# List scheduling of every engine's order in a gated attention and MLP kernel, with attention started beside the projections and phi(k) transposed by DMA

## The chip, the cores and the metric

The kernel runs on one core of a Trainium2 chip. The time is device microseconds (us) of one execution, given as the median of several runs. The program gives the core five instruction streams and fixes the order of each when it is built: PE (matrix multiply; its weight loads are listed as PEld), DVE (vector), ACT (activation functions), POOL (general purpose), SP (here it only issues DMAs). They wait for each other through semaphores. "Span" is the time from the first to the last instruction of the profiled run. It is about 2 us shorter than the reported time (256.4 against 258.4 us for the kernel before).

## The reference

The output is a gated sum of an attention branch and a token-mixing MLP. Here S = 2048 tokens, D = 448, H = 16 heads of Dh = 28, N = 4 segments of L = 512 tokens, F = 1792.

```python
def _A_ref(x, wq, wk, wv, wo, beta):          # q, k, v: x @ w, split in heads and segments
    phi = lambda t: jnp.where(t > 0, t + 1.0, jnp.exp(t))
    for s in range(N):
        p = softmax(q_s @ k_s.T * scale + causal_mask)
        a_dot = p @ v_s
        a_mem = (phi(q_s) @ M) / (phi(q_s) @ z + 1e-6)
        o = g * a_mem + (1.0 - g) * a_dot      # g = sigmoid(beta), one per head
        M = M + phi(k_s).T @ v_s
        z = z + phi(k_s).sum(0)
    return o @ wo

def _B_ref(x, w1, b1, w2, b2):                 # mixes tokens: w1 is S x F, w2 is F x S
    h = layernorm(x)
    u = gelu(einsum('bsd,sf->bdf', h, w1) + b1)
    return (einsum('bdf,fs->bds', u, w2) + b2).transpose(0, 2, 1)

g = sigmoid((x * gate_w).sum(-1))
return g * a + (1 - g) * b
```

## The kernel before

The program is first recorded as a list of operations with the buffers they read and write. Semaphore waits are derived from that list. Each engine gets its operations in the order of the text, so the hand order is the schedule:

```python
    def op(self, eng, fn, reads=(), writes=(), name=None, dma=False, group=None, out=False):
        ...                                    # dependencies from reads and writes
        self.ops.append(o)
        self.per_eng[eng].append(o)            # program order is engine order
```

First come the projections, token block by token block. phi(q) takes four instructions on three engines. phi(k) is needed with tokens on partitions, and a second projection of x by wk supplies it in that layout:

```python
    def do_q(tc, hg):
        proj_d(wq_pad, R_wqp, hg, tc, b)                                        # PE, 4 matmuls
        op("DVE", lambda e: e.tensor_copy(qs, bank(b)[:, 0:512]), ...)
        op("ACT", lambda e: e.activation(eqt[:, p, :], bank(b)[:, 0:512], ACT.Exp), ...)
        op("POOL", lambda e: e.tensor_scalar(eqt[:, p, :], eqt[:, p, :], 1.0, 0.0, op0=ALU.min, op1=ALU.max), ...)
        op("DVE", lambda e: e.scalar_tensor_tensor(phq..., qs, 0.0, eqt[:, p, :], op0=ALU.max, op1=ALU.add), ...)

    def do_kt(t):
        proj_t(wk_nat, [R_wkn], D, t, b)                                        # PE, 4 matmuls: the second K projection
        op("ACT", ... ACT.Exp from PSUM); op("POOL", ... min)
        op("DVE", lambda e: e.scalar_tensor_tensor(phk..., bank(b)..., 0.0, ekt..., op0=ALU.max, op1=ALU.add), ...)

    for tc in range(4):
        ...                                    # K, memory state, Q, V, second K, layernorm statistics
        if tc == 3:
            ln_coef()
            for t in range(NT):
                ln_apply(t)                    # 16 POOL operations, in one block
```

Then come 16 attention units (segment, head group) with three score slots each. The MLP's 448 matmuls are spread evenly among the slots. Each output tile is closed by the output projection, so attention is added last:

```python
    for n in range(NSLOT + 2):
        if n < NSLOT:
            scores(n)                          # PE scores, ACT exp of up to 128 x 2048, POOL causal mask
        if n % 3 == 1 and n >= 4:
            pv_unit(n // 3 - 1)                # PE p @ v and memory term, DVE scaling and transposes
        target = total * (n + 1) // (NSLOT + 2)
        mlp(target - pos[0])                   # the next matmuls of the MLP stream
        if y_done: ...
            wo_tile(T, MISC, range(NHG))
            final(T, MISC)                     # DVE: gate * attention + (gated MLP result)
```

The softmax here doesn't subtract the row's maximum and nothing guards it: scores larger than these inputs give would overflow.

## Time and profile before

The median is 258.97 us (258.11 to 259.32, 3 runs).

| stretch of the span, us | what runs | PE busy | clock granted to PE |
|---|---|---|---|
| 11.07 to 92 | projections, phi | 62.3 of 80.9 | 0.88 |
| 92 to 106 | layernorm applied on POOL | 9.7 of 14.0 | 0.50 |
| 106 to 244 | attention and MLP | 119.6 of 138.0 | 0.97 |

From the page of the kernel before: busy time and share of the span by engine, then three rows of the 40 equal slices (each digit is tenths of a slice; PEclk is the clock that the profile shows as granted to PE, in tenths of full speed), then the engines of the chain that ended last (followed back from the last instruction, at each step to what released it).

```profile
PE 201.7 (79%) x1377; PEld 90.4 (35%) x1389; DVE 147.3 (57%) x265; ACT 140.5 (55%) x180; POOL 83.3 (32%) x122
...
PE   0499994996795028998989984995889898899893
...
POOL 8001112301402099714443542340443223233000
PEclk9999998699799555589999998899999999999999
...
PE 39%; DVE 25%; ACT 18%; POOL 9%; issue 4%; DMA 3%; DVEq 0%; ACTq 0%
```

No engine is busy all the time, and the chain changes engine often. In slices 14 to 17 the clock row stands at 5: PE does almost nothing in the first two of them (0 and 2 in its row) and works at that clock in the other two (8 and 9). Next, the busy time of each engine in chosen stretches of the same run; the columns are stretch, length, busy time and instruction count per engine, granted clock, share of the DMA engines, GB/s:

```profile
core 0: us, PE busy (x) PEld busy (x) DVE busy (x) ACT busy (x) POOL busy (x), PEclk, DMA share, GB/s
0.00:11.07 11.07, 1.95 (x16) 1.75 (x16) 2.88 (x4) 1.28 (x1) 5.98 (x14) 1.00 0.87 251
11.07:92.00 80.93, 62.32 (x341) 30.04 (x341) 47.01 (x105) 33.31 (x74) 16.90 (x26) 0.88 0.31 74
92.00:106.00 14.00, 9.65 (x29) 2.05 (x30) 0.00 (x0) 2.34 (x2) 13.72 (x21) 0.50 0.00 1
106.00:244.00 138.00, 119.56 (x950) 52.46 (x961) 94.93 (x152) 101.40 (x101) 46.68 (x63) 0.97 0.28 79
244.00:256.40 12.40, 8.28 (x44) 4.09 (x42) 2.46 (x4) 2.17 (x3) 0.00 (x0) 1.00 0.11 37
```

And pieces of the chain of waits in order of time (start, duration, what). L410 is the max-add that ends phi(q). It comes back every 2.78 us, the latency of one pass through DVE, ACT, POOL and DVE again. L498 and L506 are layernorm on POOL; PE sits idle for 8.59 us before the first MLP matmul, waiting for L506.

```profile
...
41.45 0.69 DVE t L410
44.23 0.69 DVE t L410
...
90.05 2.95 POOL t L498
93.70 11.20 POOL t L506 x16
...
```

### The profile page before, as it was taken

To read this page: it belongs to the slowest core of one execution; us is meant where nothing else is said; L and a number is where in the kernel's file an instruction comes from. 1 tells how busy PE (TensorE), PEld (TensorE's weight loads), DVE (VectorE), ACT (ScalarE), POOL (GpSimd) and SP (SyncE) were. 2 spreads that over 40 slices of the span, in tenths; PEclk is the share of its full clock that TensorE was granted. 3 is DMA by queue.
4 is the path that set the end of the run, shared out by engine and by line. 5 is a ranking of instruction groups with operands and counts; after the bars stand their busy time and mean duration, and the time that the engine had idled before them with its cause. 6 is when DMAs were issued, how large, how long until landed. Compare 5 with 4: busy or idle time off the path is not lost.

```text
span 256.4 us, 3519 instructions
## 1 busy us (share of the span) xinstructions
PE 201.7 (79%) x1377; PEld 90.4 (35%) x1389; DVE 147.3 (57%) x265; ACT 140.5 (55%) x180; POOL 83.3 (32%) x122
## 2 busy tenths in 40 slices
PE   0499994996795028998989984995889898899893
PEld 0245551362352001233334431432343343334451
DVE  0426855944854700235567785974986677568703
ACT  0234614532641602389999986776766757756121
POOL 8001112301402099714443542340443223233000
PEclk9999998699799555589999998899999999999999
DMA  6999900000000000032632523145061460100102
GB/s 202 311 257 291 289 10 0 5 0 0 0 3 0 0 1 0 0 102 64 164 94 51 143 62 85 36 111 143 0 182 38 141 179 21 36 20 0 36 3 72
DMA packets 35908, 20.19 MB, mean 79 GB/s; under 512 B 1332, under 2 KB 35892, under 8 KB 35892
## 3 DMA queue, kind: packets, MB, share of 16 engines
q1 hardware_dynamic: 33328, 18.35, 26.5%
q10 hardware_dynamic: 2564, 1.62, 2.6%
q8 instruction: 11, 0.18, 0.3%
q14 instruction: 5, 0.04, 0.1%
HBM read 18.13 MB, written 1.84 MB: 78 GB/s over the span
## 4 chain that ended last, share of the span: by engine, by line
PE 39%; DVE 25%; ACT 18%; POOL 9%; issue 4%; DMA 3%; DVEq 0%; ACTq 0%
PE t L689 13%; ACT t L577 9%; PE t L374 6%; PE t L385 5%; PE t L656 5%; POOL t L506 4%; PE t L720 4%; DVE t L410 3%; DMA t<-in_A_wq_dram 3%; POOL t L408 3%; DVE t L402 3%; ACT t L406 3%; PE t L608 3%; PE t L568 2%; DVE t L728 2%
## 5 line engine op out<-in xcount | busy, mean ns | idle before, releaser
L577 ACT ACTIVATE t<-t 128x2048 bf16<-128x2048 f32 (+1 forms) x48 | 76.5, 1594 | 30.9 <-PE t L568 30.8
L656 PE MATMUL t<-t 128*128 128x448 bf16 x224 | 55.0, 382 | 10.4 <-POOL t L506 8.6
L689 PE MATMUL t<-t 128*128 128x448 bf16 x224 | 46.4, 353 | 0.0
L587 POOL TENSOR_SCALAR_AFFINE_SELECT t<-t 128x512 bf16<-128x512 bf16 x32 | 23.9, 748 | 50.4 <-ACT t L577 50.4
L582 POOL TENSOR_SCALAR_AFFINE_SELECT t<-t 128x512 bf16<-128x512 bf16 x32 | 24.2, 756 | 33.0 <-ACT t L577 31.9
L656 PEld LDWEIGHTS t<-t 128*128 128x128 bf16 x224 | 20.5, 101 | 38.0 <-issue 15.4
L374 PE MATMUL t<-t 112*128 112x512 bf16 x128 | 31.3, 401 | 3.3 <-DVE t L365 3.3
L385 PE MATMUL t<-t 112*128 112x449 bf16 (+1 forms) x112 | 26.7, 393 | 7.9 <-ACT t L406 6.5
L568 PE MATMUL t<-t 28*128 28x512 bf16 (+3 forms) x256 | 18.2, 319 | 16.1 <-ACT t L577 11.2
L689 PEld LDWEIGHTS t<-t 128*128 128x128 bf16 x224 | 20.2, 98 | 20.1 <-issue 2.6
L670 DVE SCALAR_TENSOR_TENSOR t<-t 128x448 f32<-128x448 f32 x14 | 9.2, 661 | 31.2 <-ACT t L667 31.1
L406 ACT ACTIVATE t<-t 128x512 bf16<-128x512 f32 x12 | 7.2, 597 | 27.6 <-DVE t L402 27.6
L728 DVE SCALAR_TENSOR_TENSOR t<-t 128x448 bf16<-128x448 f32 x16 | 10.5, 671 | 17.0 <-PE t L720 14.8
L408 POOL TENSOR_SCALAR t<-t 128x512 bf16<-128x512 bf16 x12 | 7.4, 613 | 38.6 <-ACT t L406 38.6
L374 PEld LDWEIGHTS t<-t 112*128 112x128 bf16 x128 | 12.9, 103 | 19.6 <-issue 3.6
L696 ACT ACTIVATE t<-t 128x448 bf16<-128x448 f32 x16 | 11.6, 722 | 14.7 <-PE t L689 14.7
L385 PEld LDWEIGHTS t<-t 112*128 112x128 bf16 x112 | 11.2, 105 | 21.4 <-DVE t L402 8.1
L410 DVE SCALAR_TENSOR_TENSOR t<-t 128x512 bf16<-128x512 bf16 x12 | 8.3, 692 | 17.9 <-POOL t L408 17.9
L568 PEld LDWEIGHTS t<-t 28*128 28x128 bf16 x256 | 5.2, 92 | 35.4 <-ACT t L577 21.8
L608 PE MATMUL t<-t 128*32 128x512 bf16 (+3 forms) x256 | 12.2, 312 | 6.8 <-DVE t L728 4.8
L429 POOL TENSOR_SCALAR t<-t 128x448 bf16<-128x448 bf16 x12 | 7.4, 616 | 25.9 <-ACT t L427 25.8
L402 DVE CAST t<-t 128x512 bf16<-128x512 f32 x16 | 11.0, 685 | 7.1 <-PE t L374 7.1
(70 smaller groups left out, 236.9 us busy)
## 6 DMA issues: line engine op xcount, KB each, us to landing
t<-in_B_w_dram SPq DMA_DIRECT2D x7, 1024.0 KB, 12.5
t<-in_B_w_dram SPq DMA_DIRECT2D x8, 896.0 KB, 5.1
t<-in_A_x_dram SPq DMA_DIRECT2D x4, 448.0 KB, 8.1
out_dram<-t SPq DMA_DIRECT2D x16, 112.0 KB, 1.7
t<-in_A_wk_dram ACTq DMA_DIRECT2D x1, 392.0 KB, 5.3
t<-in_A_wq_dram ACTq DMA_DIRECT2D x1, 392.0 KB, 7.9
t<-in_A_wv_dram ACTq DMA_DIRECT2D x1, 392.0 KB, 9.7
t<-in_A_wo_dram ACTq DMA_DIRECT2D x4, 98.0 KB
```

Source lines behind the costliest of these rows:

```text
L374: last = e.matmul(bank(b)[:, 0:512], w_pad[0:CK, c, hg * 128 : hg * 128 + 128], xT[0:CK, c, tc * 512 : tc * 512 + 512], start=(c == 0), st ...
L385: last = e.matmul(bank(b)[:, 0:ncol], xT[0:CK, c, t * 128 : t * 128 + 128], w[0:CK, c, 0:ncol], start=(c == 0), stop=(c == NCT - 1), skip_ ...
L402: op("DVE", lambda e: e.tensor_copy(qs, bank(b)[:, 0:512]), reads=[R_bank[b]], writes=[R_qT[hg][tc]], name=f"cpq{tc}_{hg}")
L410: op("DVE", lambda e: e.scalar_tensor_tensor(phq[:, hg, (tc - 1) * 512 : tc * 512], qs, 0.0, eqt[:, p, :], op0=ALU.max, op1=ALU.add), read ...
L568: last = e.matmul(bank(hl)[:, c0 : c0 + w_], kT[r, hg, s * 512 + j * 128 : s * 512 + j * 128 + 128], qT[r, hg, s * 512 + 128 * j : s * 512 ...
L577: op("ACT", lambda e: e.activation(pv, ps[:, 0:4, 0:w], ACT.Exp, scale=SCALE), reads=R_bank[0:4], writes=[R_P[u % 2][f]] + alias, name=f"e ...
L582: op("POOL", lambda e, d=d: e.affine_select(d, d, pattern=[[0, 4], [1, 128]], compare_op=ALU.is_ge, fill=0.0, base=0, channel_multiplier=- ...
L587: op("POOL", lambda e: e.affine_select(d, d, pattern=[[0, 4], [1, 128]], compare_op=ALU.is_ge, fill=0.0, base=0, channel_multiplier=-1), r ...
L608: last = e.matmul(bank(CTX)[32 * hl : 32 * hl + 32, 128 * j : 512], vaug[:, 4 * s + j, 32 * h : 32 * h + 32], pv[:, hl, c0 : c0 + w_], sta ...
L656: op("PE", lambda e: e.matmul(bank(b)[:, 0:D], w1c[:, st, f2 * 128 : f2 * 128 + 128], xh[:, st, :], start=(st == 0), stop=(st == NT - 1), ...
L689: op("PE", lambda e: e.matmul(bank(b)[:, 0:D], w2c[:, ft, t2_ * 128 : t2_ * 128 + 128], uT[:, ft, :], start=(ft == 0), stop=(ft == NFT - 1 ...
L728: op("DVE", lambda e: e.scalar_tensor_tensor(outst[:, p, :], bank(b)[:, 0:D], gcol[:, T : T + 1], ybw[:, T % 4, :], op0=ALU.mult, op1=ALU. ...
```

## The change

The intent is to let the program find its own overlap. Every operation gets an estimated cost and a priority class, and a list scheduler orders each engine for the whole kernel. On each engine it repeatedly takes the ready operation of the best class. The classes let attention go ahead of the projections, so its exps can start after the first quarter of them. The rest of the change gives the scheduler room and removes work:

- Buffers are laid out anew. The exps no longer lie over the transposed x and phi(k), nor the MLP's middle result over the projection weights. There are seven weight slots in place of five, and four of them reuse buffers of the projections and of phi(k).
- phi(k) comes from the K copy already in SBUF and is transposed by 12 DMAs, so the second K projection goes.
- The epsilon of the denominator is folded into a mask, and the sum of the two attention terms moves from DVE to POOL.
- The MLP's second half goes to the end, and its result y is added last.
- Nine warm-up matmuls run before the data arrives.

```diff
@@ the scheduler (cut)
+    def plan(self):
+        ...                                   # ready times from dependencies, one queue per engine
+            _, o = heapq.heappop(avail[e])    # lowest prio among the ready ones
+            ...
+            self.per_eng[e].append(o)         # this is the engine's order
@@ classes
+    P_BASE, P_ATT, P_PROJ, P_WO, P_M1, P_M2 = 0.0, 100.0, 200.0, 300.0, 400.0, 500.0
@@ phi(k) (cut)
-    def do_kt(t):
-        proj_t(wk_nat, [R_wkn], D, t, b)
-        ...
+    def do_kphi(tc, hg):
+        op("ACT", lambda e: e.activation(kphi[:, p, :], ks, ACT.Exp), ..., prio=P_PROJ + tc)
+        op("POOL", lambda e: e.tensor_scalar(kphi[:, p, :], kphi[:, p, :], 1.0, 0.0, op0=ALU.min, op1=ALU.max), ...)
+        op("DVE", lambda e: e.scalar_tensor_tensor(kphi[:, p, :], ks, 0.0, kphi[:, p, :], op0=ALU.max, op1=ALU.add), ...)
+        op("SP", lambda e: e.dma_start_transpose(phk[:, 4 * tc : 4 * tc + 4, hg * 128 : hg * 128 + 128],
+                                                 kphi[:, p, :]), ...)
@@ layernorm ranks ahead of the projections
+           reads=[R_x[t], R_rstd, R_nmr], writes=[R_x[t]], name=f"ln{t}", cost=580, prio=P_PROJ - 10)
@@ the sum of the attention terms
-            op("DVE", lambda e: e.tensor_tensor(o, oA[:, :], t2[:, 1, :], op=ALU.add), ...)
+            op("POOL", lambda e: e.tensor_tensor(o, t2[:, 0, :], t2[:, 1, :], op=ALU.add), ..., cost=1350, prio=pr)
@@ the end: attention is scaled early by ACT, the MLP result is added last
+        op("ACT", lambda e: e.activation(ag(T), bank(b)[:, 0:D], ACT.Identity, bias=b2g[:, T : T + 1],
+                                         scale=gcol[:, T : T + 1]), ...)
-        op("DVE", lambda e: e.scalar_tensor_tensor(outst[:, p, :], bank(b)[:, 0:D], gcol[:, T : T + 1],
-                                                   ybw[:, T % 4, :], op0=ALU.mult, op1=ALU.add), ...)
+        op("DVE", lambda e: e.scalar_tensor_tensor(outst[:, p, :], bank(b)[:, 0:D], omg[:, T : T + 1], ag(T),
+                                                   op0=ALU.mult, op1=ALU.add), ...)
@@ (buffers, loads, the remaining costs cut)
```

## The prediction

> **What bounds it now.** No single engine. The page gives a span of 256.4 us, PE busy 79%, DVE 57%, ACT 55%, POOL 32%. The chain of waits mixes PE 39%, DVE 25%, ACT 18%, POOL 9%: the order of work bounds. The busy times by stretch show three stages:
> - 0–92 us, projections. Each phi(q) is DVE copy, ACT exp, POOL min, DVE max-add, 2.78 us per tile on the chain, twelve times; PE stalls, its granted clock falls to 0.88.
> - 92–106 us, layernorm applied on POOL (11.2 us on the chain), PE nearly idle, clock 0.5: eight 448-column matmuls take 2.8–5.4 us, later 1.6. The Trainium skill, "TensorE: Matmul & The Clock Gate", section "What's actually happening", says that an idle window of about 3.4 us halves the clock; this trace agrees (0.50 here, 1.00 when busy).
> - 106–244 us, attention beside the MLP: 8.6 us per unit, 16 units; PE busy 119.6 of 138 us, ACT 101. Then 12 us of MLP and output.
>
> **What changes.** Removed: the second K projection, 48 matmuls (9 us of PE), and 12 eps adds (2.7 us of DVE). Added: 12 SBUF-to-SBUF transposing DMAs, 9 warm-up matmuls before data, 12 POOL adds of 512 f32 (the DVE sums, 9.5 us, go there). Moved: attention of segment 0 starts after a quarter of the projections; phi and layernorm fill gaps; all mm2 (224 matmuls) goes to the end, with a DVE add and a DMA behind each tile. Weight slots: five to seven.
>
> **Cost, by start-to-start times in the timeline** (0.19 us per 448-column matmul; ACT instructions overlap by 0.1 us, so exps take 1.77 and 0.93):
> - PE: MLP 448 x 0.19 = 85; projections 128 x 0.216 + 64 x 0.19 = 40; attention with memory term 30; output projection 12; transposes, state, mode changes 12. Sum 179 us.
> - ACT: exps 71.5, copies 17, phi exps 12.5, gelu 22, output scaling 10, rest 3: 136 us, about 131 before the last attention unit.
> - DVE about 115, POOL about 95 us in that stretch.
>
> **Sum.** First projection at about 9.5 us (11.1 before): x and wk arrive in smaller pieces, but a tanh of beta, whose small DMA took 9.9 us to land before, is ordered ahead of ACT's first copy. Everything up to the last attention unit is bounded by ACT (131) and PE (125) together; with 10% of stalls in fixed orders it ends near 152 us. Behind it only PE: 44 mm1 matmuls 8.4, output projection 3, mm2 42.5 us; then 3.5 us for add and DMA. Span 207–209, plus 2.5 us outside it as before.
>
> Predicted: **209 us**, range 198 to 224. Faster by over 2%: 0.96; within 2%: 0.025; slower: 0.015.
>
> **What would show it.** PE clock near 1.0 after 10 us; no PE gap over 3 us; first exp before 20 us; last exp at 145–160 us with ACT 85–90% busy until then; the last 45–55 us PE over 95% busy while ACT and POOL idle; PE busy 185–195 us; chain of waits mostly PE and ACT.
>
> **What would make it wrong.** The transposing DMAs: the skill, "VectorE: DVE Perf Modes", section "The three transpose paths", gives 1309 ns for one 128x128; no transfer in this trace shows it. They queue on SP behind 3 MB of weights; phi(k) is double-buffered, so late ones stall ACT, DVE, then PE, in order. If each takes over 5 us: 220 or more. DVE slowed by more POOL traffic (690 ns adds take up to 1.1 us now) would also lengthen the first stretch. If the fixed orders fit the chip better than I assume: 200.

## The result, and the profile after

The median is 223.85 us (222.83 to 224.56, 4 runs), against 258.54 us for the kernel before in the same rounds. The ratio is 0.8657, with a 95% interval of 0.861 to 0.8705. Ratios in this document divide the mean time of one kernel by that of the kernel before in the same rounds, so they are not quite the ratio of the quoted medians.

Some lines that follow are named by their line in the new kernel:

| line | operation |
|---|---|
| L491 | K and Q projections |
| L675, L684, L688 | scores, exp, causal mask |
| L711 | p @ v |
| L511 and L513 | POOL min and DVE max-add of phi(k) |
| L632 to L639 | layernorm (L633 is its power, L639 its application) |
| L774, L799 | first and second half of the MLP |

From the page of the new kernel, the rows that answer to those of before:

```profile
PE 194.6 (87%) x1343; PEld 86.7 (39%) x1350; DVE 145.3 (65%) x261; ACT 138.1 (62%) x181; POOL 105.8 (47%) x133
...
PE   7599696968866988958879898999999999999994
...
POOL 8120419999999567966484445455452000000000
PEclk9999999679996799985999999999999999999999
...
PE 52%; DVE 17%; POOL 16%; ACT 12%; issue 2%
```

The POOL row now holds 9s in slices 7 to 13, where it was busy for at most 4 tenths before, and is empty at the end, while the PE row ends in 9s. The stretches of the new kernel:

```profile
10.00:33.00 23.00, 20.85 (x134) 9.02 (x133) 18.56 (x57) 15.93 (x23) 4.61 (x7) 1.00 0.82 204
33.00:69.00 36.00, 26.34 (x221) 11.36 (x222) 26.45 (x42) 28.47 (x41) 34.61 (x43) 0.89 0.10 20
69.00:100.00 31.00, 26.11 (x209) 10.25 (x204) 25.03 (x37) 23.89 (x33) 23.47 (x28) 0.89 0.14 29
100.00:165.70 65.70, 61.26 (x478) 25.47 (x482) 51.39 (x80) 59.06 (x69) 36.10 (x42) 0.96 0.50 135
165.70:222.80 57.10, 53.95 (x284) 27.48 (x282) 19.54 (x29) 8.23 (x14) 1.26 (x1) 1.00 0.27 81
```

From 33 to 69 us POOL is busy for 34.61 of 36 us (fifth busy figure), while PE works only 26.34 of them at a mean clock of 0.89. After 165.7 us PE is busy for 53.95 of 57.10 us, while ACT (8.23) and POOL (1.26) are nearly idle. The last p @ v of attention ends at 165.65 us.

The timeline on POOL shows what fills it (start, duration, engine, line, operation, tile shapes, count):

```profile
34.69 2.92 POOL L633 TENSOR_TENSOR t<-t 128x16 f32<-128x16 f32 x1
...
39.38 3.24 POOL L639 TENSOR_SCALAR t<-t 128x448 bf16<-128x448 bf16 x4
42.58 0.63 POOL L688 TENSOR_SCALAR_AFFINE_SELECT t<-t 128x512 bf16<-128x512 bf16 x1
43.20 2.80 POOL L639 TENSOR_SCALAR t<-t 128x448 bf16<-128x448 bf16 x4
...
```

The power of layernorm (2.92 us) and its sixteen applications stand between the masks of attention. The p @ v of the second and of the fifth attention unit, on PE, wait for those masks (the bracket is the idle time before it and what ended it):

```profile
39.44 0.73 PE L711 MATMUL t<-t 128*32 128x512 bf16 x16 [2.36 <-POOL t L688]
...
68.84 1.25 PE L711 MATMUL t<-t 128*32 128x512 bf16 x16 [1.96 <-POOL t L688]
```

Another change shows in the groups of instructions (line, engine, operation, shapes, count, then busy us and mean ns). The max-add of phi(q), in the kernel before, and then the max-add of phi(k), in the new one:

```profile
L410 DVE SCALAR_TENSOR_TENSOR t<-t 128x512 bf16<-128x512 bf16 x12 | 8.3, 692 | 17.9 <-POOL t L408 17.9
```

```profile
L513 DVE SCALAR_TENSOR_TENSOR t<-t 128x512 bf16<-128x512 bf16 x12 | 11.4, 960 | 0.0
```

It is the same operation on the same shapes, and its mean duration went from 692 to 960 ns. The Trainium skill, "SBUF — State Buffer", section "SBUF: two separate sides", says that a DVE operation with two SBUF inputs and a GpSimd operation that reads SBUF exclude each other through a shared port for the whole instruction. This trace agrees in direction: with POOL busy beside it the operation is slower on average. One by one, the twelve took between 675 and 1750 ns, so some were not slowed although POOL was busy. The final add (L804), which has one PSUM input, takes 684 ns with POOL idle, against 671 before (L728), where POOL was partly at work.

### The profile page after: what moved, and what is told of

Same layout as the page of the kernel before. It is cut to its first block, busy times and chain, and to the rows that moved or that the text cites. A ratio compares the mean times of both kernels' runs of the same rounds, so it can differ in the third digit from the quotient of the medians. Undisturbed runs are those within 1.5% of the kernel's fastest.

```text
span 222.8 us, 3401 instructions
## 1 busy us (share of the span) xinstructions
PE 194.6 (87%) x1343; PEld 86.7 (39%) x1350; DVE 145.3 (65%) x261; ACT 138.1 (62%) x181; POOL 105.8 (47%) x133
## 4 chain that ended last, share of the span: by engine, by line
PE 52%; DVE 17%; POOL 16%; ACT 12%; issue 2%
PE t L799 19%; PE t L774 11%; PE t L491 7%; ACT t L684 6%; POOL t L639 6%; POOL t L688 5%; PE t L757 4%; PE t L545 3%; PE t L711 2%; DVE t L734 2%; DVE t L736 2%; DVE t L784 2%; PE t L675 2%; PE t L447 2%; DVE t L744 2%
## 5 line engine op out<-in xcount | busy, mean ns | idle before, releaser
L684 ACT ACTIVATE t<-t 128x2048 bf16<-128x2048 f32 (+1 forms) x48 | 77.2, 1608 | 5.4 <-PE t L675 5.3
L688 POOL TENSOR_SCALAR_AFFINE_SELECT t<-t 128x512 bf16<-128x512 bf16 x64 | 47.5, 747 | 39.2 <-ACT t L684 38.1
L774 PE MATMUL t<-t 128*128 128x448 bf16 x224 | 50.6, 359 | 2.4 <-ACT t L781 1.3
L799 PE MATMUL t<-t 128*128 128x448 bf16 x224 | 42.5, 352 | 0.0
L491 PE MATMUL t<-t 112*128 112x512 bf16 x128 | 35.8, 425 | 4.2 <-DVE t L484 2.1
L774 PEld LDWEIGHTS t<-t 128*128 128x128 bf16 x224 | 20.7, 99 | 24.2 <-issue 7.2
L804 DVE SCALAR_TENSOR_TENSOR t<-t 128x448 bf16<-128x448 f32 x16 | 10.9, 684 | 29.0 <-PE t L799 29.0
L799 PEld LDWEIGHTS t<-t 128*128 128x128 bf16 x224 | 21.9, 98 | 20.5 <-DVE t L789 0.2
L738 POOL TENSOR_TENSOR t<-t 128x512 bf16<-128x512 f32 x12 | 16.8, 1401 | 13.3 <-DVE t L736 13.3
L675 PE MATMUL t<-t 28*128 28x512 bf16 (+3 forms) x256 | 17.8, 312 | 5.8 <-ACT t L684 5.7
L491 PEld LDWEIGHTS t<-t 112*128 112x128 bf16 x128 | 12.2, 106 | 21.8 <-issue 6.8
L725 DVE STREAM_TRANSPOSE t<-t 128x512 f32<-128x512 f32 x16 | 11.3, 709 | 11.4 <-PE t L711 11.2
L711 PE MATMUL t<-t 128*32 128x512 bf16 (+3 forms) x256 | 12.7, 322 | 6.9 <-POOL t L688 6.8
L545 PE MATMUL t<-t 112*128 112x449 bf16 x64 | 15.9, 385 | 1.5 <-DVE t L524 1.3
L757 PE MATMUL t<-t 128*128 128x448 bf16 x64 | 15.1, 368 | 1.5 <-DVE t L744 1.3
L503 ACT ACTIVATE t<-t 128x512 bf16<-128x512 f32 x16 | 9.6, 605 | 8.9 <-PE t L491 8.9
L639 POOL TENSOR_SCALAR t<-t 128x448 bf16<-128x448 bf16 x16 | 14.7, 927 | 0.5 <-PE t L471 0.5
L744 DVE STREAM_TRANSPOSE t<-t 128x512 bf16<-128x512 bf16 x16 | 11.2, 703 | 4.7 <-POOL t L738 4.6
L675 PEld LDWEIGHTS t<-t 28*128 28x128 bf16 x256 | 5.2, 92 | 22.9 <-ACT t L684 16.3
L511 POOL TENSOR_SCALAR t<-t 128x512 bf16<-128x512 bf16 x12 | 9.2, 768 | 8.1 <-ACT t L509 8.1
```

Of the source, the lines that this page charges most:

```text
L491: last = e.matmul(bank(b)[:, 0:512], w_pad[0:CK, c, hg * 128 : hg * 128 + 128], xT[0:CK, c, tc * 512 : tc * 512 + 512], start=(c == 0), st ...
L545: last = e.matmul(bank(b)[:, 0 : D + 1], xT[0:CK, c, t * 128 : t * 128 + 128], wvx[0:CK, c, :], start=(c == 0), stop=(c == NCT - 1), skip_ ...
L639: op("POOL", lambda e: e.tensor_scalar(xh[:, t, :], xh[:, t, :], rstd[:, t : t + 1], nmr[:, t : t + 1], op0=ALU.mult, op1=ALU.add), reads= ...
L675: last = e.matmul(bank(hl)[:, c0 : c0 + w_], kT[r, hg, s * 512 + j * 128 : s * 512 + j * 128 + 128], qT[r, hg, s * 512 + 128 * j : s * 512 ...
L684: op("ACT", lambda e: e.activation(pv, ps[:, 0:4, 0:w], ACT.Exp, scale=SCALE), reads=R_bank[0:4], writes=[R_P[u % 2][f]], name=f"exp{n}", ...
L688: op("POOL", lambda e, d=d: e.affine_select(d, d, pattern=[[0, 4], [1, 128]], compare_op=ALU.is_ge, fill=0.0, base=0, channel_multiplier=- ...
```

## The experiments

All twelve runs gave correct results. Unless said otherwise, a run is the new kernel with the edit shown. The runs name four explanations for the time that was missed:

- **A:** POOL's backlog from 33 to 69 us holds attention up.
- **B:** DVE sets the pace after 69 us, and DVE and POOL slow each other.
- **C:** the orders are fixed from wrong durations.
- **D:** the half clock of PE costs the time.

### e1_ln_dve and e2_ln_late: layernorm off POOL, or later on POOL

```diff
 e1:
-        op("POOL", lambda e: e.tensor_scalar(xh[:, t, :], xh[:, t, :], rstd...   cost=580, prio=P_PROJ - 10)
+        op("DVE", lambda e: e.tensor_scalar(xh[:, t, :], xh[:, t, :], rstd...    cost=250, prio=P_PROJ - 10)
 e2:
-  coefficients prio=P_BASE, application prio=P_PROJ - 10
+  coefficients prio=P_PROJ + 8, application prio=P_PROJ + 9
```

> Layernorm apply (16 ops, 14.7 us on POOL) goes to DVE[...]. Theory A (POOL's backlog from 33 to 69 us, 34.6 of 36 us busy, holds up the masks and with them the attention): the last attention unit ends 5 to 9 us sooner, time 215 to 219 us. Rival B (DVE is the limit before 120 us; POOL's backlog only shifts waiting): under 2 us gained, or slower, since DVE gets more work.

> The same layernorm work stays on POOL but ranks behind phi(q) and phi(k). Theory A in the form 'it is the order on POOL': masks and phi come earlier, 2 to 6 us gained, the first MLP matmul later than 85.7 us. If it is the amount of POOL work and not its order: within 1.5 us of 223.9 or slower, because the MLP starts later and the attention stage has less to fill PE with.

e1 measured 220.78 us (ratio 0.8538, 0.8508 to 0.8568) and e2 220.75 us (0.8523, 0.8497 to 0.8548). Against the new kernel's 0.8657 that is a gain of 3.1 us for e1 (0.0119 of 258.6) and of 3.5 us for e2; from here on gains are worked out in this way, and the 95% intervals make them uncertain by about 1.5 us. Since e2 leaves all the work on POOL (34.54 of 36 us busy from 33 to 69 us), the order is enough for its gain. But the path that theory A named does not show: the last p @ v ends at 164.38 us in e1 and 165.04 us in e2, after 165.65 us, and not 5 to 9 us sooner. What ends sooner is the first half of the MLP (169.21 and 170.44 us, after 177.56 us).

### e3_o_dve and e4_min_dve: moving work between POOL and DVE

```diff
 e3:
-            op("POOL", lambda e: e.tensor_tensor(o, t2[:, 0, :], t2[:, 1, :], op=ALU.add), ...  cost=1350
+            dv(lambda e: e.tensor_tensor(o, t2[:, 0, :], t2[:, 1, :], op=ALU.add), ...           650
 e4:
-        op("POOL", lambda e: e.tensor_scalar(... 1.0, 0.0, op0=ALU.min, op1=ALU.max)  # phi(q), phi(k)
+        op("DVE", lambda e: e.tensor_scalar(... 1.0, 0.0, op0=ALU.min, op1=ALU.max)
```

> Undoes one part: the 12 sums of the two attention terms go back from POOL (16.8 us) to DVE (about 0.65 us each, 8 us in all). There is none of them before segment 1, so the stretch 33 to 69 us stays. Rival B (DVE limits 69 to 120 us, 43 of 51 us busy): 3 to 6 us slower. If POOL-DVE interference or POOL latency is what costs there, it is equal or up to 3 us faster.

> The 24 min operations of phi (18.7 us on POOL) go to DVE. Theory A: POOL's backlog shrinks by half, 3 to 7 us gained. Rival B: DVE gets 24 more instructions[...], time equal or up to 4 us slower.

e3 measured 226.03 us (0.8734, 0.871 to 0.8757): 2.0 us slower, so moving the sums to POOL was a small gain. e4 measured 221.97 us (0.8585, 0.8545 to 0.8625): 1.9 us faster. Both effects are barely clear of the noise and lie between what the two theories said. On DVE a sum took 0.85 us and a min 0.38 us. Relieving one of the two engines loads the other. POOL's busy time from 33 to 69 us fell to 24.34 us in e4 and 23.81 us in e1, from 34.61 us, without the gain that theory A expected, so POOL alone does not set the pace of that stretch.

### e5_fill: keep PE's clock up

After the plan is made, short matmuls of the identity with itself are put in front of six PE operations that wait. They write to a PSUM bank that the next operation overwrites.

```diff
     sch.plan()
+    FILL = {"pv1": (CTX, 24), "prd2_": (CTX, 14), "prd3_": (CTX, 12), "pv4": (CTX, 20), "pv7": (CTX, 16), "prt15": (None, 16)}
+    ...  last = e.matmul(bank(b)[:, 0:128], ident[:, :], ident[:, :], start=True, stop=True, ...)
```

> 102 short matmuls of the identity with itself are put into the six longest PE gaps of the new kernel between 36 and 100 us (1.0 to 1.5 us each, less than the gap), so that the activity does not fall; results unchanged. Theory D (the four stretches at half clock, 20.5 us of the trace, cost about 10 us of PE time and that is part of the missing 15 us): the half clock mostly disappears and 4 to 9 us are gained. Rival A+B (POOL until 69 us and DVE until 112 us set the pace, PE would only wait longer): the clock rises, the gaps grow, under 2 us gained.

It measured 223.81 us (0.8666, 0.863 to 0.8701), the same time, while the mean clock rose from 0.954 to 0.977. The stretches of this run, to be compared with those of the new kernel above:

```profile
10.00:33.00 23.00, 20.85 (x130) 8.73 (x129) 17.32 (x51) 15.46 (x23) 4.40 (x7) 0.88 0.81 203
33.00:69.00 36.00, 28.70 (x278) 14.86 (x276) 27.53 (x44) 29.11 (x41) 33.83 (x42) 0.95 0.10 20
69.00:100.00 31.00, 26.46 (x257) 12.41 (x258) 25.39 (x37) 24.39 (x34) 23.55 (x29) 1.00 0.15 31
```

In the last two the clock is at 0.95 and 1.00 (it was 0.89 in both), and POOL is as full as before (33.83 of 36 us). Before 33 us it fell from 1.00 to 0.88, ahead of the first added matmul (37.60 us). Counted as time at half clock, the trace has about 10 us where the new kernel had about 20. Theory D finds no support: the time did not move, give or take 1.5 us, so the low clock from 33 to 100 us cost little of its own. It is not excluded altogether, since half of that time remains, and two of the four executions had a mean clock of 0.962, which the new kernel reached too.

### e6_kt: the second K projection back

```diff
-        op("SP", lambda e: e.dma_start_transpose(phk..., kphi[:, p, :]), ...)
+        last = e.matmul(bank(b)[:, 0:512], xT[0:CK, c, t * 128 : t * 128 + 128], wk_pad[0:CK, c, :], ...)  # 4 per token tile
+        ...   # exp from PSUM, min on POOL, max-add from PSUM into phk
```

> Undoes one part: phi(k) comes from a second K projection with tokens on partitions (48 matmuls of 512 columns, 10.4 us of PE at 0.216 us) as before, in place of the 12 transposing DMAs; all else and the scheduler stay. If the removed PE work is gain on the critical path: 8 to 13 us slower. If POOL and DVE set the pace in that stretch and PE has slack: under 4 us slower.

It measured 235.71 us (0.9108, 0.9082 to 0.9133): 11.7 us slower by the ratios (0.0451 of 258.6). That fits the 10.4 us of PE work, but the run does not isolate it: the second K projection also takes PSUM banks that the scores need, and the first scores, which wait for a max-add of phi(k), come at 40.83 us where they came at 21.04 us. How the 11.7 us divide between the two is not shown.

### e7_no_overlap: projections ahead of attention

```diff
-    P_BASE, P_ATT, P_PROJ, ... = 0.0, 100.0, 200.0, ...
+    P_BASE, P_ATT, P_PROJ, ... = 0.0, 250.0, 200.0, ...
```

> Undoes one part: projections rank ahead of attention, so the exps start later; list scheduling, transposing DMAs and the order of the end stay. If the overlap of attention with the projections is the main gain: 12 us slower or more, as ACT (131 us of work before the last attention unit) starts its exps later. If list scheduling and the removed work are the main gain: within 5 us of 223.9, since the MLP can fill PE beside attention as before.

It measured 217.21 us (0.8402, 0.8376 to 0.8429): 6.6 us faster than the new kernel, which lies outside both expectations. The part of the change that should have been its main gain costs time when the rest is in place. Starting attention early adds its masks and its DVE work to the stretch in which POOL and DVE already carry phi and layernorm (from 33 to 69 us POOL is busy 34.61 us in the new kernel and 29.38 us here). That this is the reason is argued, not tested. The first MLP matmul, which could keep PE busy, comes at 85.66 us in the new kernel and at 75.65 us here.

This run has a fault of its own. In its timeline POOL runs twelve layernorm applications in a row (8.75 us), the max-add of phi(k) on DVE has waited 8.86 us for POOL when it starts, and PE has waited 7.61 us for DVE:

```profile
...
37.47 8.75 POOL L639 TENSOR_SCALAR t<-t 128x448 bf16<-128x448 bf16 x12
...
46.84 2.86 DVE L513 SCALAR_TENSOR_TENSOR t<-t 128x512 bf16<-128x512 bf16 x1 [8.86 <-POOL t L511]
...
50.35 1.89 PE L491 MATMUL t<-t 112*128 112x512 bf16 x4 [7.61 <-DVE t L524]
...
```

### e8_recost: plan with the measured durations

```diff
-  ln 580, phi min 627, phi max-add 683, power 250, oa 650, om 650, garg 630
+  ln 900, phi min 760, phi max-add 930 and 880, power 2920, oa 790, om 750, garg 720
```

> The scheduler plans with the durations that the profile of the new kernel shows in place of its own guesses: layernorm apply 0.90 us for 0.58, phi min 0.76 for 0.63, phi max-add 0.93 and 0.88 for 0.68, the power 2.92 for 0.25, the two scalings of attention 0.79 and 0.75 for 0.65, gelu argument 0.72 for 0.63. Theory C (orders fixed from too short durations cause the stalls): 3 to 8 us gained. Rival: the amount of work per engine and its rank set the pace, not the guesses: within 2 us.

It measured 226.36 us (0.8759, 0.874 to 0.8778), 2.6 us slower. Theory C falls in this form. The stretch from 33 to 69 us did improve:

```profile
33.00:69.00 36.00, 31.52 (x265) 13.37 (x263) 25.56 (x44) 34.88 (x52) 32.31 (x43) 0.98 0.08 16
```

PE is busy for 31.52 us (26.34 in the new kernel), and the first MLP matmul comes at 67.63 us. But the projections now last until 110.29 us (101.35 before), and between 100 and 140 us PE is busy for 32.00 us after 35.92. Better durations alone did not give a better order under these classes. With the classes of e7 or e9 they were not run, so that rival stays open.

### e9_noov_lnlate and e10_noov_lndve: e7 with layernorm moved

```diff
 e9 = e7 + e2,   e10 = e7 + e1
```

> e7 and e2 together: projections rank before attention, and layernorm apply ranks behind phi(q) and phi(k) on POOL. Theory E (in the run without overlap, POOL's pow and 12 layernorm ops from 33.5 to 46.2 us hold phi(k), DVE for 8.9 us and PE for 7.6 us): that gap goes, 209 to 213 us. Rival (the MLP needs all of layernorm, so later layernorm means a later first MLP matmul than 75.7 us, and that sets the time): 215.5 to 220 us.

> e7 and e1 together: projections first, layernorm apply on DVE (it took 0.56 us each there, 8.1 us in all, for 12 to 15 us on POOL). Theory E: the gap of 7.6 us goes and layernorm is over earlier, 208 to 213 us. Rival (DVE is then the pace, it has 27.6 of 31 us already from 69 to 100 us): 215 us or more.

e9 measured 215.8 us (0.8342, 0.832 to 0.8363), a further 1.5 us, and is the best of the variants that keep the new operations. e10 measured 219.05 us (0.8472, 0.8451 to 0.8493), 1.8 us slower than e7. The rival's number was closer both times. Its mechanism for e9 was not: the first MLP matmul came at 72.57 us, sooner than in e7 (75.65 us). The wait of 7.6 us shrank to 5.3 us in e9, so theory E was only half put to the test there. In e10 it is gone (no wait of PE for another engine exceeds 2.9 us), and the time rose all the same.

### e11_sched_only: the scheduler alone, on the old operations

Everything of the kernel before stays: its operations, shared buffers, second K projection and evenly spread MLP. The order of every engine changes, DMA issues included. The new `finalize` comes along and drops waits that others already cover, so that the trace has 63 semaphore instructions where it had 125; what that alone is worth was not run. The new `plan` is put in, the priority of an operation is its place in the hand order, and the costs are taken from the durations in the profile of before or from the new kernel's cost helpers.

```diff
-        self.per_eng[eng].append(o)                 # hand order
+        prio = len(self.ops)                        # hand order is only the priority
+        cost, mode, nbytes = guess(eng, name, dma)
...
+    sch.plan()
     totals = sch.finalize()
```

> The kernel before with one part of the change alone: its own operations, buffers and second K projection, but the order of each engine from the new list scheduler, with the hand order as priority. If list scheduling by itself brings most of the gain: 235 us or less. If the gain comes from freeing the operations from one another (own buffers and banks, less PE work, phi from SBUF copies, layernorm not in one block): above 248 us.

It measured 207.3 us (207.17 to 207.75; ratio 0.8022, 0.8004 to 0.8041). That is 51 us less than the kernel before and 16.4 us less than the whole change (0.0635 of 258.5). It still has the PE work of the second K projection. From its page, with the stretches below:

```profile
PE 190.5 (93%) x1389; PEld 88.0 (43%) x1389; DVE 149.6 (73%) x265; ACT 139.3 (68%) x180; POOL 84.0 (41%) x122
...
PE   0699999999988999999999989899999999999992
...
POOL 8300304589996244334534442542342341432000
PEclk9999999999999999999999999999999999999999
...
```

```profile
8.60:66.70 58.10, 56.49 (x337) 29.19 (x337) 46.63 (x100) 30.62 (x71) 30.87 (x43) 1.00 0.47 114
66.70:190.00 123.30, 120.69 (x977) 51.36 (x978) 94.43 (x151) 104.63 (x107) 46.69 (x65) 1.00 0.31 89
190.00:205.40 15.40, 11.35 (x61) 5.68 (x58) 5.85 (x11) 2.89 (x4) 0.00 (x0) 1.00 0.10 31
```

PE is busy 56.49 of 58.10 us during the projections (62.3 of 80.9 before), because other work now fills the passes through DVE, ACT and POOL. All of it belongs to the projections and the memory state: the first score matmul starts at 66.74 us and the first MLP matmul at 67.40 us. The applications of layernorm run from 45.56 to 63.43 us, beside the projections, and no longer in a block behind them. Of the 51 us, about 37 are gained here (94.93 us from 11.07 to 106 us before, 58.10 now). PE is busy 120.69 of 123.30 us during attention and MLP, with the clock at 1.00 throughout; that stretch took 138 us before. POOL is busy 30.87 of those 58.10 us; in the same stretch of the new kernel it is busy 36.93 us and PE 47.37. Then PE-heavy MLP and ACT-heavy attention run side by side to the end, and ACT is busy 104.63 of 123.30 us.

The groups of this run also show the two forms of phi's max-add side by side. L552 has two SBUF inputs, L573 takes one of its inputs from PSUM:

```profile
L552 DVE SCALAR_TENSOR_TENSOR t<-t 128x512 bf16<-128x512 bf16 x12 | 10.1, 866 | 2.5 <-POOL t L550 2.5
L573 DVE SCALAR_TENSOR_TENSOR t<-t 128x448 bf16<-128x448 f32 x12 | 7.3, 613 | 2.5 <-POOL t L571 2.5
```

In the kernel before, the PSUM form took 622 ns, so it is undisturbed here (613), while the SBUF form is again slowed (866, from 692).

### e12_mix: the old mix of MLP and attention, with the new operations

This is e9, with the MLP ranked evenly among the attention units rather than behind them.

```diff
-               prio=P_M1 + ft)                      -  prio=P_M2 + T)                 -  pr = P_WO + T
+               prio=P_ATT + 16.5 * i / 408.0)       # i: place in the stream of 448   +  pr = P_ATT + T + 4.6
```

> The run with projections first and layernorm late (215.8 us), with one thing changed: the MLP matmuls no longer rank behind all attention but are spread evenly among the 16 attention units, as the hand order had them, and each output projection ranks behind its own unit. Operations, buffers and transposing DMAs are those of the new kernel. Theory F (what the new kernel loses against list scheduling of the old operations, 207.3 us, is the ranking: attention in front starves PE, then PE runs alone for 57 us): 203 to 209 us, PE clock 1.0 after 75 us, no PE-only end over 25 us. Rival (the loss lies in the new operations, POOL sums and phi from SBUF, and in their interference on DVE and POOL): 213 us or more.

It measured 220.64 us (218.23 to 221.75; 0.8551, 0.8518 to 0.8584): 5.4 us slower than e9 by the ratios. One of its four executions (221.75 us) is slow, as it is 1.6% above the fastest; its clock of 0.959 lies among those of the others (0.953 to 0.961). The three fast ones average 219.84 us, still 4.2 us above e9 (215.64). The theory that the ranking of the MLP behind attention loses the 8.3 us between e9 and e11 falls in this form. The stretch from 69 to 100 us, first in e9, then in e12:

```profile
69.00:100.00 31.00, 27.50 (x246) 12.27 (x245) 25.76 (x44) 26.74 (x38) 14.04 (x20) 1.00 0.58 140
```

```profile
69.00:100.00 31.00, 26.84 (x194) 12.60 (x192) 20.84 (x37) 18.86 (x30) 9.12 (x13) 0.94 0.73 176
```

With MLP matmuls let in front, ACT's busy time falls from 26.74 to 18.86 of 31 us, and PE does not gain for it (26.84 after 27.50). The even spread that suits the old operations starves the exps here. The likely reason, not tested by itself, is that projections still run in this stretch, so that PE's time is shared three ways.

## Why the prediction was right, and where its sum was off

Direction, size class and range held: 209 us was predicted with a range of 198 to 224, and 223.85 was measured. That is 0.15 us inside the range, with one execution of four (224.56) outside, so that the range held by luck. The gain was 35 us where 50 were expected. Point by point:

- **What bounded the kernel: right.** "The order of work bounds" is what e11 shows. Reordering alone, with every operation kept, removes 51 us.
- **The beginning: right in the number.** First projection predicted at about 9.5 us, measured at 9.81 us. The tanh of beta did wait for its DMA (2.48 us, until 7.17 us), but PE's first transposes started only at 7.01 us, and ACT's first copy then waited for PE. The smaller pieces are not shown to be the reason: with the old loads, e11 starts its first projection at 8.64 us.
- **The end: right.** Behind the last attention unit 8.4 + 3 + 42.5 + 3.5 = 57.4 us were predicted, and the trace has 222.80 - 165.65 = 57.15 us.
- **The term that was mis-sized.** The step was: "Everything up to the last attention unit is bounded by ACT (131) and PE (125) together; with 10% of stalls in fixed orders it ends near 152 us." It ended at 165.65 us, 13.7 us later. The terms of the sum add to a span of 209.4 us (the stated 207 to 209 is a little less), and 222.8 us were measured, so that this term is the whole miss. The sum treated that time as one stage with two limits. The trace has several engines that are nearly full in turn: POOL from 33 to 69 us, DVE from 80 to 120 us (18.75 and 18.28 of each 20 us), and PE with ACT only after that. In those 155.8 us ACT was busy 127.4 us, 82% and not the 85 to 90% predicted. The experiments put 3.5 us of the loss on layernorm ahead of phi (e2), and 8.1 us on that together with the early start of attention (e9). The rest is not traced to a single cause. Nor does the end of attention alone fix the time: in e8 it came at 158.21 us, 7.4 us sooner, and the run took 2.6 us longer.
- **PE's clock: wrong, without an effect that shows.** "Near 1.0 after 10 us" was expected and the mean was 0.954, although no gap exceeded 3 us, as predicted. e5 raised it part of the way and the time did not move.
- **The last stretch: nearly right.** "PE over 95% busy while ACT and POOL idle" for 45 to 55 us became 53.95 of 57.10 us (94.5%).
- **The chain: partly wrong.** "Mostly PE and ACT" became PE 52%, DVE 17%, POOL 16%, ACT 12%. The first exp came at 21.6 us and not before 20. The last one (started at 162.4 us) missed the predicted 145 to 160 us slightly.
- **Transposing DMAs: the feared cost did not come.** The Trainium skill, "VectorE: DVE Perf Modes", section "The three transpose paths", gives 1309 ns for one 128x128. A transfer of four such blocks landed 2.4 us (median) after its issue:

```profile
t<-t SPq DMA_TRANSPOSE x12, 2.4
```

- **DVE slowed by POOL: right as a risk, not in the sum.** The max-add rose from 692 to 960 ns.
- **PE busy 185 to 195 us: right** (194.6).
- **Not tested:** the new buffers, the warm-up matmuls, the folded epsilon and adding y last, each by itself.

The measured effects do not add up to a list of independent parts. Within the new kernel, putting back the second K projection in place of the transposing DMAs costs 11.7 us (e6), and the overlap of attention with the projections costs 6.6 us (e7). On the old operations, the scheduler alone gives more than everything together (e11). Why the best variant with the new operations (e9, 215.8 us) stays 8.3 us behind e11 is open. The traces say where, not why: from 8.60 to 66.70 us PE is busy for 56.49 us in e11 and for 46.91 us in e9, whose projections end at 84.45 us and not at 65.74. Candidates are POOL's larger load (about 101 us busy after 84), the slower max-adds from SBUF, projections that run into the attention stage, and planned durations: e11 plans with measured ones (2.9 us for the power of layernorm), e9 with guesses (0.25 us). None was isolated. Of all versions run, e11 is the fastest and beats both kernels.

## What to carry to other kernels

Try the scheduler on the old program first, with the hand order as its priority. Here the reordering alone gave 51 us, and the rewrite that came with it gave 16 us back, about half of that through its ranks (e9). When you sum engine loads for an overlapped stage, sum them per stretch and include the small engines: starting a stage earlier can cost time where the engines that it needs are already full, as POOL nearly was here. A low clock or an idle PE in such a stretch can be a symptom, so test it by filling the gaps before you count it as a cost.

## What the Trainium skill lacked or had wrong

- "TensorE: Matmul & The Clock Gate", section "What's actually happening": the table has the clock halved after at least one idle window of about 3.4 us. In the new kernel the mean clock was 0.954 over 222.8 us. Counted as time at half clock that is 0.046 x 222.8 / 0.5, about 20 us, although the longest wait of PE in the timeline after the start was 2.36 us. So stretches in which PE is idle only in part lost clock too. The page's section "A second HAM failure mode: psum-queue depth-cycling" describes such short idles; neither says from what share on.
- The same section does not say that the lower clock may cost little where PE waits anyway. In the trace of e5 the mean clock rose from 0.954 to 0.977 and the median stayed (223.81 after 223.85 us, uncertain by about 1.5 us).
- "Perfetto Trace Analysis", section "Optimization Strategy", advises to interleave regimes whose most-contended engine differs. e11, where layernorm on POOL runs beside the projections, is in line with it (207.3 us). It lacks the warning that interleaving can cost time where the regimes share an engine: with attention beside the projections POOL was busy 34.61 of 36 us, and ranking the projections first was 6.6 us faster. That POOL is the reason was not isolated.
- "SBUF — State Buffer", section "SBUF: two separate sides", states the exclusion between DVE and GpSimd but gives no measured time for a bf16 operation with two SBUF inputs beside a busy POOL. Here 692 ns became 960 ns on average (675 to 1750 ns).
- "VectorE: DVE Perf Modes", section "The three transpose paths", has only a single 128x128. For SBUF to SBUF with four blocks in one DMA this case shows 2.4 us from issue to landing.
